# Linear attention with decay, then an MLP: group 0 scaled from SBUF, group 3 turned by TensorE, four output buffers, a new written order

## The chip, the cores and the metric

The kernel runs on one core of one Trainium2 chip. The metric is the device time of one execution in microseconds (us). A core has TensorE (PE, the matrix engine; its weight loads are shown as PEld), VectorE (DVE), ScalarE (ACT), GpSimd (POOL), SyncE (SP, which here only issues DMAs) and DMA engines that all queues share. The engines run at the same time; each executes its own list of instructions in order and waits only where data or a buffer isn't ready.

## The reference

`r`, `k`, `v` have the shape (4 sequences, 8 heads, 768 steps, 48); `w` and `u` have one value for each head and channel.

```
for t in range(S):
    cur     = outer(u * k[t], v[t])
    y[t]    = r[t] @ (state + cur)
    state   = w * state + outer(k[t], v[t])
x = y as (3072 tokens, 384)
h = x @ w_in                       # 384 -> 2048
g = h if h >= 1, 0 if h <= -1, else (h+1)^2/4
out = g @ w_out                    # 2048 -> 384
```

## The kernel before

**Tiling.** The 768 steps are cut into 6 chunks of 128 (`C`). The 4 sequences are taken two at a time (`UNITS = 2`). So there are 12 groups, `g = 2*chunk + pair`, and 24 units, `n = 2*g + j`; a unit is 128 tokens of one sequence with all 8 heads. Group 3 is the "fourth group": chunk 1, second pair of sequences.

**Attention of one group.** The recurrence over steps becomes matrix products inside a chunk. Loads of R, K and V (`LR`, `LK`, `LV`, issued by SP, line 252). R and K are scaled with powers of `w` that depend on the step (`Rs`, `Ks`, tables `Wup` and `Wdn`, line 271) and turned, so that channels lie on the partitions: either by TensorE (`TR`, `TK`, `T`, line 319) followed by a copy out of PSUM (`cR`, `cK`, `c`, line 111), or by a transposing DMA on SP's queue (`RT`, `KT`, line 307). `A` (line 359) are the products of turned K and turned R, `AT` the same under the triangular mask (DVE). `Y` (lines 421 and 427) adds `AT` times V and turned R times the state. The term with `u` goes by the diagonal: `KU = K*u`, `RKU = R*KU`, `us` sums it per head, `B` multiplies it with V (cast to bf16 by `V` on ACT), and `y`/`yg` adds it to `Y`. `Sp` (line 394) is the new part of the state, `Tm`/`Tmg` and `decayg` update the state, `sbf`/`sbfg` cast it to bf16.

**MLP of one group.** y is turned (`X` on TensorE with the copy `xc`, or `xcg` by a transposing DMA). `m g.q` (line 464) is a quarter of the first product (12 matmuls), `r`, `s`, `g` are the activation (mostly ACT, ACT, DVE), `M g.jq` (line 499) a quarter of the second product for one unit (4 matmuls). `og` copies the result out of PSUM into a buffer `o`, `stg` stores it. `WI` and `WO` load the weights, cast to bf16 on the way, from POOL's queue.

**The start.** `ln`, `bw`, `WupS`, `WdnS` build the two tables in SBUF from `w`, and `Wup`, `Wdn` build the same in PSUM for group 0, so that group 0 can be scaled early. `bu`, `uS` spread `u`.

**The order** is written out by hand in `ORDER`: the program is emitted word by word, and each engine gets its instructions in that order. A word is the step, the group or unit, a letter for the engine after `=` (V is DVE, A is ACT, G is POOL), and after `/` the PSUM buffers: banks `b0` to `b3` for the first two groups' small tiles, pairs `p0`, `p1` from the beginning, and pairs `p2`, `p3` that take the place of the four banks later. Zn stands for n matmuls of zeros into a buffer that nobody reads.

**Buffers** are counted in `SLOTS`. The one that counts here is `"o": 2`: an `og` has to wait until the store of the `og` two before it has landed.

```
def do_Rs(e, b, g, j=None):
    t = flat(Wup) if g else tiles["up_t"]      # up_t: the table in PSUM
def do_og(e, b, g):
    copy(e, make("o", ("o", g), ...), tiles["op", g][:, :, :DO])
```

Of the kernel before, what the change touches and what calls it, by code (L numbers as in the profile page):

```python
# [21 lines left out]


ORDER = """
Zs/0 LK0.0 LR0.0 LK0.1 LR0.1 LR1.0 LR1.1 ln Z19 bw/2 WupS bu/1 Wdn/0 Ks0.1=V Wup/1 uS=A KU0.1=G Ks0.0=V Z5 TK0/3
Rs0.0=V TR0/1 cK0=V Rs0.1=V TK1/0 cK1=A RKU0.1=V LV0.0 LV0.1 KU0.0=V RKU0.0=G WdnS us0.1 cR0=A Z14 A0/23 us0.0 AT0.0
TR1/0 cR1=A Z4 A1/01 Rs1.1=V WI0 WI1 LK1.0 LK1.1 V0.0 wq/2 wE B0.0=G Rs1.0=G LV1.0 LV1.1 AT1.0 AT0.1 Z4 Y0/2 WI2 TR3/0
LK2.0 AT1.1 Ks1.0=G cR3=A Ks1.1=V Z6 TK3/1 cK3=V V0.1 B0.1=G LR2.0 LR2.1 V1.0 y0 TR2/3 cR2=V LK2.1 Z2 A3/01 AT3.0 X0/2
xc0=V KU1.1=G Y1/3 y1 KU1.0=G RKU1.0=G TK2/0 cK2=V Z2 X1/2 AT3.1 A2/30 AT2.1 wC=A Sp1/1 Tm1 xc1=A m0.0/0 r0.0=A s0.0=A
m0.1/1 r0.1=A LK3 us1.0 AT2.0 RKU1.1=G us1.1 Sp2/0 Tm2 LR3 Y2/0 V1.1 Sp3/1 s0.1=A B1.0=V Y3/3 y2 X2/2 xc2=A g0.0  # L30
m0.2/0 r0.2=A B1.1=G y3 X3/0 Sp0/2 g0.1 s0.2=A m0.3/1 r0.3=A s0.3=A Tm3 Tm0 xc3=V m1.2/3 m1.0/2 g0.2 WO0 WO1 Rs2=G
Ks2=G m1.1/0 r1.2=V g0.3 m1.3/1 KU2=G RKU2=G s1.2=A g1.2 LV2.0 LV2.1 LV3 M0.00/3 M0.10 M0.01 r1.0=A s1.0=A g1.0 r1.3=A
s1.3=A M0.11 g1.3 M1.00/2 sbf1=A sbf0=A M1.10 Rs3=G M0.12 M0.13 T4/1 r1.1=A s1.1=A M0.02 M0.03 Ks3=V KT3 KU3=G c4=A
T5/1 c5=A g1.1 us2 V2 B2=G A4/0 AT4 M1.11 RT3 LR4 LK4 A5/1 AT5 og0=A LR5 M1.12 M1.13 Y4/0 Y5 yg2 sbf2=A V3 RKU3=G
M1.01 AA3/13 AT6 X4/0 xc4=A M1.02 X5/0 xc5=A M1.03 og1=A LK5 AT7 Y6/1 m2.0/0 sbf3=A us3 Rs4=G RT4 Sp4/2 Sp5 Tmg2
r2.0=A s2.0=A B3=G Y7 yg3 xcg3 m2.1/3 r2.1=A m2.3/2 LV4 m2.2/1 Ks4=G KT4 g2.0 M2.00/0 M2.10 s2.1=A g2.1 M2.01 M2.11
LV6 r2.2=V m3.1/3 stg0 KU4=G RKU4=G LK6 LR6 r2.3=A s2.3=A s2.2=A decayg2=G g2.3 r3.1 m3.0/2 g2.2 M2.02 M2.03 Sp6/1 Sp7
us4 s3.1=A KU5=G M2.12 Ks5=G r3.0 g3.1 M2.13 s3.0=A KT5 Tmg3 og2=A Rs5=G m3.2/3 g3.0 LV5 V4 AA4/01 AT8 sbfg2=A
decayg3=G m3.3/2 RT5 AT9 B4=G M3.00/0 stg1 r3.2 s3.2=A M3.01 Y8/1 Y9 RKU5=G r3.3 g3.2 yg4 xcg4 s3.3=A V6 M3.10 M3.02
g3.3 KU6=G V5 sbfg3=A M3.11 LK10 stg2 us5 M3.12 M3.03 LR7 AA5/21 AT10 M3.13 Rs6=G og3=A m4.0/3 AT11 B5=G r4.0 LK7  # L40
m4.1/2 s4.0=A Y10/0 Y11 m4.2/1 r4.1 s4.1=A yg5 Ks6=G xcg5 RKU6=G m4.3/0 g4.0 RT6 M4.00/3 M4.10 r4.2 s4.2=A g4.1 Rs7=G
M4.11 Sp8/2 Sp9 KT6 M4.01 g4.2 LV7 LR8 M4.02 m5.1/1 LR9 r4.3 Tmg4 s4.3=A g4.3 decayg4=G us6 B6=G r5.1 KU7=G AA6/02
AT12 M4.03 LK8 sbfg4=A AT13 M4.12 M4.13 m5.0/0 s5.1=A RT7 g5.1 Ks7=G og4=A Y12/2 Y13 m5.2/1 r5.0 s5.0=A m5.3/3 yg6
xcg6 g5.0 RKU7=G Sp10/2 Sp11 r5.2 s5.2=A M5.00/0 M5.10 Ks8=G KT7 Tmg5 M5.11 LK9 decayg5=G g5.2 M5.01 M5.02 us7 m6.1/2
r5.3 s5.3=A g5.3 stg3 V7 LR11 B7=G r6.1 AA7/13 AT14 M5.12 KU8=G KT8 sbfg5=A s6.1=A M5.13 AT15 Rs8=G M5.03 og5=A m6.0/1
g6.1 LV8 r6.0 KU9=G RT8 s6.0=A Rs9=G Y14/3 Y15 Sp12/0 yg7 m6.2/2 m6.3/3 Sp13 xcg7 r6.2 stg4 g6.0 M6.00/1 s6.2=A Tmg6
decayg6=G r6.3 RT9 g6.2 M6.10 RKU8=G LR10 M6.11 Ks9=G M6.01 s6.3=A g6.3 stg5 M6.12 m7.1/0 AA8/32 M6.02 V8 r7.1 AT17
s7.1=A M6.13 KT9 M6.03 AT16 m7.0/2 sbfg6=A Sp14/3 Sp15 LV10 KU10=G us8 B8=G og6=A stg6 g7.1 r7.0 m7.2/1 s7.0=A Tmg7
LV9 Rs11=G g7.0 Y16/0 Y17 decayg7=G m7.3/3 yg8 r7.2 s7.2=A M7.00/2 xcg8 M7.10 Ks10=G r7.3 g7.2 s7.3=A g7.3 M7.11 M7.01
M7.02 V10 AA9/01 AT18 RT11 RKU9=G V9 M7.12 AT19 KT10 sbfg7=A M7.13 RKU10=G LK11 m8.0/3 Rs10=G M7.03 us9 r8.0 us10  # L50
og7=V s8.0=A g8.0 B9=G m8.1/1 r8.1 Y18/0 Y19 RT10 B10=G s8.1=A yg9 m8.2/2 r8.2 KU11=G xcg9 m8.3/3 s8.2=A g8.1 M8.00/0
LV11 M8.10 r8.3 M8.01 Sp16/1 g8.2 Sp17 Tmg8 M8.11 M8.12 stg7 m9.0/2 s8.3=A decayg8=G g8.3 AA10/31 AT21 M8.13 r9.0
M8.02 AT20 s9.0=A M8.03 m9.1/1 V11 sbfg8=A Y20/3 Y21 g9.0 Ks11=G og8=A yg10 xcg10 m9.2/0 r9.1 KT11 s9.1=A M9.00/3 r9.2
s9.2=A g9.1 m9.3/2 RKU11=G stg8 g9.2 M9.10 M9.11 r9.3 Sp18/1 Sp19 Tmg9 s9.3=A M9.01 M9.02 g9.3 decayg9=G us11 m10.0/0
r10.0 B11=G AA11/12 M9.12 M9.13 AT23 s10.0=A M9.03 sbfg9=A AT22 og9=V m10.1/2 stg9 Y22/1 Y23 g10.0 m10.2/3 r10.1
M10.00/0 s10.1=A r10.2 yg11 xcg11 g10.1 M10.10 m10.3/1 s10.2=A g10.2 r10.3 s10.3=A M10.01 M10.11 m11.1/2 M10.12 M10.02
g10.3 r11.1 m11.0/3 s11.1=A g11.1 M10.13 m11.2/1 r11.0 m11.3/2 s11.0=A r11.2 s11.2=A g11.0 M10.03 M11.10/3 og10=V
M11.11 r11.3 stg10 g11.2 M11.00/0 M11.01 M11.02 s11.3=A g11.3 M11.12 M11.13 M11.03 o11.1=A st11.1 o11.0=A st11.0
"""
# [14 lines left out]
def kernel(  # L74
# [193 lines left out]
    def product(e, out, a, b, g, j):  # L268
        j0, j1 = by_unit(g, j)
        part = lambda x: x.rearrange("p (b h) d -> p b h d", b=UNITS)[:, j0:j1]  # L270
        engines[e].tensor_mul(part(out)[:, :, :, :D], part(a), rep(b, j1 - j0) if len(b.shape) == 3 and b.shape[1] == H else part(b))  # L271
# [295 lines left out]
```

## Time and profile before

| | |
|---|---|
| three runs | 178.55 us median (178.06 to 178.93) |
| profiled execution | 177.88 us, of which the span from first to last instruction is 176.1 us |
| TensorE | 163.8 us busy (93%), 1638 matmuls, 1638 weight loads |
| DVE | 131.0 us busy (74%), 149 instructions |
| ACT | 129.3 us busy (73%), 150 instructions |
| POOL | 114.9 us busy (65%), 83 instructions |
| first product | 576 matmuls, 68.8 us; second product: 384 matmuls, 68.5 us |
| mean granted TensorE clock | 0.990 of full speed |

Busy time is the union of the spans of an engine's instructions. A matmul's span holds its way through the array, so spans overlap and the mean of one is more than what a matmul adds to a dense stream; what a stream takes is read from start to start. "Idle before, releaser" in a row says how long an engine stood before an instruction and what ended that.

### The profile page before, as it was taken

Reading aid. Unit: us, or ns where it says so; the run is one execution under the profiler, and the core shown is the slowest. Engines: PE = TensorE matmul, PEld = TensorE weight load, DVE = VectorE, ACT = ScalarE, POOL = GpSimd, SP = SyncE. Lnnn points to the kernel's source line nnn. Section 1 sums busy time; section 2 is a strip of 40 time slices with the busy share of each in tenths; the row PEclk is TensorE's granted clock in tenths of the full one; section 3 lists DMA queues with packets and bytes.
Section 4 is the critical chain, followed back from the end, with each engine's and each line's share of the span. In section 5 each row is a group of like instructions: output and inputs, shape, how many; then the busy total and the mean of one; then the engine's idle time right before and its main releaser. Section 6 shows DMA issues by size and latency. Waiting matters only on the chain.

```text
span 176.1 us, 3979 instructions
## 1 busy us (share of the span) xinstructions
PE 163.8 (93%) x1638; PEld 129.0 (73%) x1638; DVE 131.0 (74%) x149; ACT 129.3 (73%) x150; POOL 114.9 (65%) x83
## 2 busy tenths in 40 slices
...
GB/s 113 196 183 189 202 184 190 207 204 195 160 187 161 177 262 153 240 266 163 174 204 168 179 254 176 217 263 231 183 111 178 45 48 149 4 134 2 2 90 92
DMA packets 105703, 28.78 MB, mean 163 GB/s; under 512 B 100946, under 2 KB 104788, under 8 KB 105684
## 3 DMA queue, kind: packets, MB, share of 16 engines
...
q8 instruction: 13, 0.21, 0.6%
...
q10 hardware_dynamic: 4, 0.00, 0.0%
HBM read 20.45 MB, written 4.72 MB: 143 GB/s over the span
## 4 chain that ended last, share of the span: by engine, by line
PE 51%; DMA 20%; SPq 15%; ACT 4%; DVE 4%; issue 2%; POOL 1%; ACTq 0%; POOLq 0%
PE hp L464 25%; PE op L499 20%; SPq L252 14%; DMA Ri<-in_r_dram 8%; DMA out_dram<-o 8%; DMA RT<-Rs 2%; DVE g L487 2%; DMA xT<-y 2%; PE A L359 2%; ACT pt L475 2%; PE Y L427 2%; PE Y L421 1%; ACT sq L484 1%; PE Sp L394 1%; POOL Rs L271 1%
## 5 line engine op out<-in xcount | busy, mean ns | idle before, releaser
L487 DVE SCALAR_TENSOR_TENSOR g<-sq,hp 128x1024 bf16<-128x1024 bf16 x48 | 58.4, 1218 | 17.1 <-ACT sq L484 16.8
L464 PE MATMUL hp<-xT,w_in 128*128 128x256 bf16 x576 | 68.8, 273 | 1.0 <-DMA xT<-y 0.8
L499 PE MATMUL op<-w_out,g 128*128 128x384 bf16 x384 | 68.5, 326 | 0.2 <-DVE g L487 0.2
L464 PEld LDWEIGHTS <-w_in 128*128 128x128 bf16 x576 | 61.9, 114 | 4.5 <-DMA xT<-y 1.4
L475 ACT ACTIVATE pt<-hp 128x1024 f32<-128x1024 f32 x46 | 46.9, 1019 | 19.1 <-PE hp L464 19.1
L499 PEld LDWEIGHTS <-g 128*128 128x128 bf16 x384 | 35.9, 98 | 22.4 <-DVE g L487 1.2
L484 ACT ACTIVATE sq<-pt 128x1024 bf16<-128x1024 f32 x46 | 48.7, 1058 | 1.4
L368 DVE TENSOR_TENSOR AT<-A,umask 128x1024 bf16<-128x1024 f32 x20 | 23.6, 1220 | 8.2 <-PE A L359 8.0
L271 POOL TENSOR_TENSOR Rs<-Ri,Wup 128x768 bf16<-128x768 f32 (+1 forms) x11 | 19.4, 1760 | 9.7 <-DMA Ri<-in_r_dram 9.7
L271 POOL TENSOR_TENSOR KU<-Ki,u_sb 128x768 f32<-128x768 f32 (+1 forms) x13 | 21.2, 1635 | 4.7 <-ACT u_sb L111 4.7
L271 POOL TENSOR_TENSOR RKU<-Ri,KU 128x768 f32<-128x768 f32 (+1 forms) x13 | 21.2, 1638 | 1.9 <-DVE KU L271 1.7
L405 POOL TENSOR_TENSOR state<-Tm,wCm 128x768 f32<-128x768 f32 x8 | 14.6, 1831 | 11.7 <-DVE Tm L402 11.7
L302 POOL TENSOR_TENSOR V<-Vb,diag 128x768 f32<-128x768 bf16 (+1 forms) x13 | 17.2, 1330 | 5.6 <-ACT Vb L111 4.5
L271 POOL TENSOR_TENSOR Ks<-Ki,Wdn 128x768 bf16<-128x768 f32 (+1 forms) x10 | 17.9, 1786 | 2.2 <-DMA Ki<-in_k_dram 2.1
L439 DVE TENSOR_TENSOR y<-Y,V 128x768 bf16<-128x768 f32 x10 | 9.6, 956 | 5.7 <-POOL RKU L271 2.4
L293 DVE TENSOR_REDUCE diag<-RKU 128x16 f32<-128x768 f32 (+1 forms) x14 | 11.6, 831 | 0.6 <-POOL RKU L271 0.6
L111 ACT COPY o<-op 128x768 f32<-128x768 f32 (+1 forms) x10 | 7.4, 737 | 6.3 <-PE op L499 3.3
L111 ACT CAST Vb<-Vi 128x768 bf16<-128x768 f32 (+1 forms) x14 | 10.2, 736 | 1.5 <-DMA Vi<-in_v_dram 1.5
L427 PE MATMUL Y<-Vb,AT 128*128 128x48 bf16 x192 | 10.5, 185 | 0.6 <-DVE state L398 0.6
L427 PEld LDWEIGHTS <-AT 128*128 128x128 bf16 x192 | 9.3, 97 | 1.4 <-issue 0.8
L402 DVE TENSOR_TENSOR Tm<-Sp,state 128x768 f32<-128x768 f32 x8 | 7.6, 955 | 1.5 <-PE Sp L394 1.4
L111 ACT CAST state_bf<-state 128x768 bf16<-128x768 f32 (+1 forms) x12 | 8.5, 720 | 0.0
...
## 6 DMA issues: line engine op xcount, KB each, us to landing
...
w_out<-in_moe_w_out_dram POOLq DMA_DIRECT2D x2, 768.0 KB, 10.2
Ki<-in_k_dram SPq DMA_DIRECT2D x6, 192.0 KB, 4.7
Ri<-in_r_dram SPq DMA_DIRECT2D x6, 192.0 KB, 4.3
Vi<-in_v_dram SPq DMA_DIRECT2D x6, 192.0 KB, 4.6
```

The costliest lines, as they stand in the source:

```text
L111: nc.scalar.copy(out, in_) if e == "A" else engines[e].tensor_copy(out, in_)
L252: nc.sync.dma_start(out=t[:, j0 * H : j1 * H, :], in_=source(x, g, j0, j1))
L271: engines[e].tensor_mul(part(out)[:, :, :, :D], part(a), rep(b, j1 - j0) if len(b.shape) == 3 and b.shape[1] == H else part(b))
L302: engines[e].tensor_mul(t[:, hs, :], tiles["V", g][:, hs, :], tiles["diag", g][:, hs].unsqueeze(2).to_broadcast([P, n, D]))
L368: nc.vector.tensor_mul(t.rearrange("p i n t -> p (i n) t"), tiles["A", n].rearrange("p i (n t) -> p (i n) t", t=P), umask.unsqueeze(1).to_ ...
L405: engines[e].tensor_mul(states[g % BP], tiles["Tm", g], flat(wCm).unsqueeze(1).to_broadcast([P, UNITS, DM]))
L427: nc.tensor.matmul(Y[:, h * D : (h + 1) * D], AT[:, i, p, :], V[:, j * H + h, :], start=(c == 0), stop=True, skip_group_check=True,)
L464: nc.tensor.matmul(hp[:, f, :], w_in_sb[wi][:, i, wo * FG * P + f : (wo + 1) * FG * P : FG], tiles["xT", g][:, :, i, :], start=(i == 0), s ...
L475: nc.scalar.activation(t, tiles["hp", g, q], AF.Relu, bias=0.5, scale=0.5)
L484: nc.scalar.activation(t, p, AF.Square)
L487: nc.vector.scalar_tensor_tensor(out=make("g", ("g", g, q), [P, FG, TOK], BF16), in0=tiles["sq", g, q], scalar=1.0, in1=tiles["hp", g, q], ...
L499: nc.tensor.matmul(tiles[key][:, k, :DO], tiles["g", g, q][:, f, j * P : (j + 1) * P], w_out_sb[wi][:, wo, f * DO : (f + 1) * DO], start=( ...
```

## The change

- Group 0's `Rs` reads the table `Wup` in SBUF, since the word `Wup/1`, which made the copy of it in PSUM, is gone. `Ks` of group 0 still reads its table in PSUM.
- Group 3 (units 6 and 7) is turned by TensorE: `T6`, `T7`, copied by `c6`, `c7` on ACT. The two transposing DMAs `RT3` and `KT3` are gone.
- `"o"` has 4 buffers, not 2.
- The whole order is new. Idle matmuls: 67 (19, 4, 9, 7, 2, 7, 8, 3, 8), which were 56 (19, 5, 14, 4, 4, 6, 2, 2). Some steps have another engine: `RKU0.0`, `KU0.1`, `B0.0`, `Rs1.0`, `KU1.0`, `RKU2`, `KU3`, `cR3`, `xc2`, `xc4`, `xc5`, `og3`, `og6`, `r1.1` and `r2.3` are now on DVE; `RKU0.1`, `Ks1.1`, `B1.0` on POOL; `cK2`, `xc0`, `r2.2`, `og7` on ACT.

```
-Zs/0 LK0.0 LR0.0 LK0.1 LR0.1 LR1.0 LR1.1 ln Z19 bw/2 WupS bu/1 Wdn/0 Ks0.1=V Wup/1 uS=A KU0.1=G Ks0.0=V Z5 TK0/3
-Rs0.0=V TR0/1 cK0=V Rs0.1=V TK1/0 cK1=A RKU0.1=V LV0.0 LV0.1 KU0.0=V RKU0.0=G WdnS us0.1 cR0=A Z14 A0/23 us0.0 AT0.0
-TR1/0 cR1=A Z4 A1/01 Rs1.1=V WI0 WI1 LK1.0 LK1.1 V0.0 wq/2 wE B0.0=G Rs1.0=G LV1.0 LV1.1 AT1.0 AT0.1 Z4 Y0/2 WI2 TR3/0
 ...
+Zs/1 LV0.0 LR0.0 LR0.1 ln LK0.0 Z19 bw/3 bu/0 WupS LK0.1 V0.0 Rs0.0=V LV0.1 Rs0.1=V LR1.0 WdnS Wdn/2 Z4 TR1/1 uS=A
+TR0/3 cR0=A cR1=A KU0.0=V Ks0.0=V RKU0.0=V KU0.1=V Z9 TK0/1 cK0=V LV1.0 RKU0.1=G WI0 Ks0.1=V us0.0 B0.0=V LK1.0 Z7
+TK1/1 cK1=A LK1.1 A0/32 LR1.1 WI1 AT0.1 Z2 A1/10 LV1.1 LK2.0 wq/2 Rs1.0=V AT1.1 V0.1 V1.0 wE Ks1.1=G AT0.0 us0.1 Z7
+Y0/0 wC=A B0.1=G AT1.0 Z8 Y1/2 TK3/3 TR2/1 y0 LR2.0 y1 X0/0 Ks1.0=G LK2.1 xc0=A cR2=V WI2 Z3 X1/1 xc1=A KU1.0=V Sp1/2
+Rs1.1=V Z8 TR3/0 Tm1 TK2/1 cK2=A cK3=V m0.0/0 cR3=V RKU1.0=G KU1.1=G A2/20 Sp2/1 r0.0=A m0.1/1 RKU1.1=G AT2.0 s0.0=A
+Tm2 us1.1 AT2.1 g0.0 r0.1=A Y2/2 A3/31 us1.0 V1.1 s0.1=A Sp3/0 AT3.1 Sp0/1 AT3.0 B1.0=G y2 Y3/3 LR2.1 g0.1 WO0 m0.3/0
+LR3 B1.1=G y3 LK3 WO1 X2/2 xc2=V Ks2=G KU2=G r0.3=A X3/3 Tm0 m0.2/1 xc3=V s0.3=A r0.2=A Tm3 m1.1/2 g0.3 s0.2=A m1.2/3
+r1.1=V g0.2 m1.0/0 s1.1=A m1.3/1 g1.1 r1.0=A LV2.0 s1.0=A sbf2=A M0.00/2 r1.2=V g1.0 M0.10 M0.11 s1.2=A M0.01 r1.3=A
+Rs2=G T4/0 c4=A M0.12 M0.13 sbf0=A g1.2 RKU2=V LV2.1 M0.02 A4/3 us2 M0.03 s1.3=A Rs3=G og0=A sbf1=A M1.00/0 M1.01
+M1.10 T5/2 g1.3 Ks3=V LV3 LK4 c5=A M1.11 KU3=V AT4 LR5 M1.12 RKU3=G A5/1 M1.13 V2 AT5 LR4 T7/2 T6/3 sbf3=A Y4/1 Y5
+B2=G us3 c7=A M1.02 M1.03 yg2 KU4=G c6=A LV4 X4/2 Sp4/1 X5/3 og1=A xc4=V Sp5 A6/2 xc5=V LK5 V3 A7/0 m2.0/3 AT6 B3=G
+AT7 m2.1/2 r2.0=A Ks4=G Tmg2 Y6/0 Y7 s2.0=A yg3 RKU4=G m2.2/1 g2.0 r2.1=A xcg3 s2.1=A g2.1 m2.3/0 r2.2=A Rs4=G M2.00/3
+KU5=G M2.10 KT4 s2.2=A LK7 M2.11 V4 m3.1/2 r2.3=V RT4 g2.2 s2.3=A g2.3 r3.1 decayg2=G M2.01 m3.0/1 LV6 stg0 s3.1=A us4
+M2.12 Rs5=G g3.1 r3.0 LK6 Sp6/0 Sp7 M2.02 M2.03 Ks5=G s3.0=A M2.13 sbfg2=A Tmg3 AA4/20 g3.0 V6 KT5 AT8 RKU5=G m3.2/1
+og2=A RT5 AT9 Y8/2 r3.2 m3.3/3 us5 LV5 Y9 s3.2=A B4=G decayg3=G M3.00/0 r3.3 s3.3=A yg4 M3.01 g3.2 xcg4 M3.10 M3.11
 ...
+s10.1=A og9=V xcg11 m10.3/3 r10.2 g10.1 stg9 s10.2=A r10.3 g10.2 s10.3=A M10.00/0 M10.10 M10.11 M10.01 m11.1/1 g10.3
+m11.0/2 r11.1 M10.02 r11.0 m11.2/3 s11.1=A M10.12 s11.0=A g11.1 M10.13 M10.03 r11.2 g11.0 s11.2=A og10=V m11.3/1
+M11.10/2 stg10 g11.2 M11.11 r11.3 M11.00/0 M11.01 s11.3=A M11.12 g11.3 M11.02 M11.03 M11.13 o11.0=A st11.0 o11.1=A
+st11.1

-SLOTS = {... "xT": 3, "pt": 3, "sq": 3, "g": 13, "o": 2}
+SLOTS = {... "xT": 3, "pt": 3, "sq": 3, "g": 13, "o": 4}

 def do_Rs(e, b, g, j=None):
-        t = flat(Wup) if g else tiles["up_t"]
+        t = tiles["up_t"] if g == 0 and "up_t" in tiles else flat(Wup)
 def do_Ks(e, b, g, j=None):
-        t = flat(Wdn) if g else tiles["dn_t"]
+        t = tiles["dn_t"] if g == 0 and "dn_t" in tiles else flat(Wdn)
```

In the order before, the corresponding stretch of groups 2 to 4 reads, cut to what the prediction speaks of:

```
... Rs3=G M0.12 M0.13 T4/1 r1.1=A s1.1=A M0.02 M0.03 Ks3=V KT3 KU3=G c4=A
T5/1 c5=A g1.1 us2 V2 B2=G A4/0 AT4 M1.11 RT3 LR4 LK4 A5/1 AT5 og0=A LR5 ... Y4/0 Y5 yg2 sbf2=A V3 RKU3=G
M1.01 AA3/13 AT6 X4/0 ... LK5 AT7 Y6/1 m2.0/0 ... RT4 ... xcg3 ... LV4 ... KT4
LV6 ... stg0 ... LK6 LR6 ... og2=A ... KT5 ... Rs5=G m3.2/3 g3.0 LV5 V4 AA4/01 ... RT5
...
M11.11 r11.3 stg10 g11.2 M11.00/0 M11.01 M11.02 s11.3=A g11.3 M11.12 M11.13 M11.03 o11.1=A st11.1 o11.0=A st11.0
```

More of the change, by code (lines that the diff above doesn't have):

```diff
@@ L24 @@
 ORDER = """
-Zs/0 LK0.0 LR0.0 LK0.1 LR0.1 LR1.0 LR1.1 ln Z19 bw/2 WupS bu/1 Wdn/0 Ks0.1=V Wup/1 uS=A KU0.1=G Ks0.0=V Z5 TK0/3
-Rs0.0=V TR0/1 cK0=V Rs0.1=V TK1/0 cK1=A RKU0.1=V LV0.0 LV0.1 KU0.0=V RKU0.0=G WdnS us0.1 cR0=A Z14 A0/23 us0.0 AT0.0
-TR1/0 cR1=A Z4 A1/01 Rs1.1=V WI0 WI1 LK1.0 LK1.1 V0.0 wq/2 wE B0.0=G Rs1.0=G LV1.0 LV1.1 AT1.0 AT0.1 Z4 Y0/2 WI2 TR3/0
-LK2.0 AT1.1 Ks1.0=G cR3=A Ks1.1=V Z6 TK3/1 cK3=V V0.1 B0.1=G LR2.0 LR2.1 V1.0 y0 TR2/3 cR2=V LK2.1 Z2 A3/01 AT3.0 X0/2
-xc0=V KU1.1=G Y1/3 y1 KU1.0=G RKU1.0=G TK2/0 cK2=V Z2 X1/2 AT3.1 A2/30 AT2.1 wC=A Sp1/1 Tm1 xc1=A m0.0/0 r0.0=A s0.0=A
@@ L30 @@
[L30 to L58, printed above, removed]
+Zs/1 LV0.0 LR0.0 LR0.1 ln LK0.0 Z19 bw/3 bu/0 WupS LK0.1 V0.0 Rs0.0=V LV0.1 Rs0.1=V LR1.0 WdnS Wdn/2 Z4 TR1/1 uS=A
```

18 lines of the change are left out of this document (17 added, 1 removed).

## The prediction

> **What bounds the kernel now.** I read the page's shares first, then busy time by stretches, then TensorE's waits, then the timeline round each wait. The stretches:
>
> ```profile
> PE 163.8 (93%) x1638; PEld 129.0 (73%) x1638; DVE 131.0 (74%) x149; ACT 129.3 (73%) x150; POOL 114.9 (65%) x83
> ...
> 8.40:19.90 11.50, 9.64 (x121) 7.81 (x120) 10.16 (x20) 5.20 (x12) 10.03 (x11) 0.85 1.28 189
> 19.90:30.00 10.10, 8.26 (x97) 7.89 (x95) 8.53 (x15) 7.43 (x9) 6.27 (x7) 1.00 1.05 189
> 30.00:50.00 20.00, 19.15 (x196) 13.54 (x195) 15.35 (x15) 15.15 (x20) 12.05 (x8) 1.00 1.23 192
> 50.00:82.00 32.00, 30.26 (x316) 24.87 (x314) 23.71 (x23) 25.66 (x29) 29.26 (x18) 1.00 1.23 207
> 82.00:167.20 85.20, 84.42 (x852) 67.40 (x851) 65.98 (x62) 69.09 (x73) 54.73 (x32) 1.00 0.72 143
> ```
>
> The first row gives busy time and share of the whole span. The columns of the others are length, then busy time of PE, PEld, DVE, ACT and POOL, PE's granted clock, the DMA share and GB/s. From 82 us on TensorE stands for 0.78 us in 85.2: there the kernel is bound by its matmuls, whose number stays. An order can win only what TensorE loses before: 1.84 us in 19.9 to 30, 0.85 in 30 to 50, 1.74 in 50 to 82; further the time until the first product starts at 19.9 us, and the tail behind the last matmul. In 8.4 to 19.9 the fullest engine is DVE (10.16 of 11.5 us), so the start is set by DVE's list. TensorE's waits, two answers (19.9 to 82 us, then 82 to the end):
>
> ```profile
> PE A L359 <- DMA RT<-Rs: 1.5, 2, 0.8
> PE Sp L394 <- ACT Vb L111: 1.0, 1, 1.0
> PE A L359 <- ACT o L111: 0.8, 1, 0.8
> PE Y L427 <- DVE state L398: 0.6, 1, 0.6
> ...
> PE hp L464 <- DMA xT<-y: 0.6, 1, 0.6
> ```
>
> **The change part by part.** The profiled execution took 177.88 us, 1.78 more than its span of 176.1, and 0.67 less than the runs' median of 178.55. I sum against the execution and take the difference to the median.
>
> *Start: Rs of group 0, loads, idle matmuls, engines.* The rows:
>
> ```profile
> 6.48 0.50 ACT L111 COPY u_sb<-up 128x384 f32<-128x384 f32 x1
> ...
> 8.20 0.54 DVE L271 TENSOR_TENSOR Rs<-Ri,up_t 128x384 bf16<-128x384 f32 x1
> 8.65 0.55 DVE L271 TENSOR_TENSOR RKU<-Ri,KU 128x384 f32<-128x384 f32 x1
> ...
> 11.85 0.55 DVE L271 TENSOR_TENSOR Rs<-Ri,Wup 128x384 bf16<-128x384 f32 x1
> ...
> 12.31 1.88 DVE L373 TENSOR_TENSOR AT<-A,umask 128x512 bf16<-128x512 f32 x3
> ...
> 14.11 1.40 DVE L271 TENSOR_TENSOR Ks<-Ki,Wdn 128x384 bf16<-128x384 f32 x1
> 14.14 0.80 POOL L243 DMA_DIRECT2D w_in<-in_moe_w_in_dram  x1
> ...
> 14.97 1.39 POOL L271 TENSOR_TENSOR Ks<-Ki,Wdn 128x384 bf16<-128x384 f32 x1
> ...
> 19.90 2.78 PE L464 MATMUL hp<-xT,w_in 128*128 128x256 bf16 x24
> ...
> 24.49 1.21 DVE L487 SCALAR_TENSOR_TENSOR g<-sq,hp 128x1024 bf16<-128x1024 bf16 x1
> ...
> 25.75 1.47 PE L464 MATMUL hp<-xT,w_in 128*128 128x256 bf16 x12 [0.16 <-DVE g L487]
> ...
> 34.34 5.46 PE L499 MATMUL op<-w_out,g 128*128 128x384 bf16 x32
> ```
>
> Rs from SBUF costs 0.55 us as against 0.54 from PSUM: nothing. `uS` has one ACT instruction more ahead of it (`V0.0`, `WdnS`, `Wdn` for `Wdn`, `Wup`), so at about 0.5 us each it ends near 7.5 instead of 6.98, and `KU0.0` on DVE starts near 7.6. K0.0 moves from the first to the fourth place of SP's queue and K0.1 from the third to the fifth; by the landings of these places
>
> ```profile
> Ri<-in_r_dram SPq DMA_DIRECT2D x1, 192.0 KB, 4.2
> ...
> Ri<-in_r_dram SPq DMA_DIRECT2D x1, 192.0 KB, 4.4
> ```
>
> (us from issue, at 2.71 and 3.54) they land at 6.9 and 7.9: in time for 7.6 and for `KU0.1` near 9.0. From 7.6 DVE has no idle place in the new list. The SBUF instructions start 0.45 to 0.5 us apart (8.20, 8.65), `AT` 0.63 (1.88 / 3), copies about 0.4. Fourteen items to `y0` (`KU0.0`, `Ks0.0`, `RKU0.0`, `KU0.1`, `cK0`, `Ks0.1`, `us0.0`, `B0.0`, `AT0.1`, `Rs1.0`, `AT1.1`, `AT0.0`, `us0.1`, `AT1.0`): 10 x 0.45 to 0.5 + 4 x 0.63 = 7.0 to 7.5, `y0` at 14.6 to 15.1; then `y1`, `cR2`, `KU1.0`, `Rs1.1` until about 17.1, `TR3`, `TK2`, and m0.0 at about 17.6, 2.3 us earlier than 19.90. Most of that is lost again: ten items follow up to `AT3.0` (`Tm1`, two copies, `AT2.0`, `Tm2`, `us1.1`, `AT2.1`, `g0.0` of 1.21, `us1.0`, `AT3.1`), and A2 has to wait for m0.0, g0.0 for ACT; I get `AT3.0` done at 24.5, Y3, and m0.3 at 25.0, where m0.2 stood at 25.75. Then X3 waits for `y3`, m0.2 runs near 27.0, four m of 1.3 (two take 2.78 with the way through the array), and M0.00 comes at about 33.6 against 34.34. I take 0.7 us. Bounds: +2.3, if all of the early m0.0 stays; -0.9, if one DVE instruction is stretched as `Ks1.1` was (1.40 where 0.55 is usual, 0.85 more) and one POOL instruction delays what DVE waits for.
>
> The eleven more idle matmuls lie in TensorE's waits for DVE and cost nothing there; with cover gone they cost 11 x 0.1. The w_in parts: the third is moved behind `B0.1` and `Ks1.0` on POOL, from 14.14 to about 16.2.
>
> *T6, T7 for RT3, KT3.* The rows:
>
> ```profile
> 39.63 0.39 PE L319 MATMUL T<-ident,Rs 128*128 128x128 bf16 x4
> 39.85 0.39 PE L319 MATMUL T<-ident,Ks 128*128 128x128 bf16 x4
> ...
> 40.28 1.01 ACT L111 COPY TT<-T 128x1024 bf16<-128x1024 bf16 x1 [0.59 <-PE T L319]
> ...
> 47.09 0.62 PE L359 MATMUL A<-RT,KT 48*128 48x128 bf16 x16 [0.80 <-DMA RT<-Rs]
> ```
>
> Four transposes take 0.22 us (39.63 to 39.85), so sixteen add 0.9 us of matmuls; the wait of 0.80 us for RT3 goes. Net 0.1 us lost. Bounds: 0.9 lost if the new place waits as long; 0.8 won if the transposes fill a wait. `c6`, `c7` are two of 1.01 us on ACT, which has 4.85 us idle in 30 to 50; behind them on ACT stand `og1` and `V3`, and A7 (pair 0) waits for `og1`: with cover gone, up to 1.0. On SP two transposes go and LK4, LR5, LR4, LV4 move up. DVE takes `RKU2`, `KU3` from POOL; idle in 30 to 50: 4.65 us.
>
> *Four output buffers.* The rows:
>
> ```profile
> 57.30 2.51 SPq L307 DMA_TRANSPOSE KT<-Ks  x1
> ...
> 60.53 1.43 SPq L518 DMA_DIRECT2D out_dram<-o  x1
> ...
> 65.33 0.80 ACT L111 COPY o<-op 128x768 f32<-128x768 f32 x1 [1.37 <-DMA out_dram<-o]
> ...
> 66.18 0.62 PE L359 MATMUL A<-RT,KT 48*128 48x128 bf16 x16 [0.83 <-ACT o L111]
> ...
> 166.32 6.01 PE L499 MATMUL op<-w_out,g 128*128 128x384 bf16 x36
> ...
> 172.77 0.48 ACT L111 COPY o<-op 128x384 f32<-128x384 f32 x1 [0.57 <-DMA out_dram<-o]
> ```
>
> The first store was issued at 60.53, `og2` waited for it to land, and A of group 4 waited 0.83 us for `og2`, whose PSUM it takes. With four buffers `og2` waits for no store: 0.8 us. Next late there would be KT4, issued at 57.30 behind RT4 and eight us before A. Bounds 0 to 0.8. At the end `o11.0` no longer waits 0.57 us; the last matmuls end at 166.32 + 6.01 = 172.33, so the copy can start 0.4 us earlier.
>
> *SP's queue before A of group 5.* The rows:
>
> ```profile
> 67.86 1.54 SPq L252 DMA_DIRECT2D Vi<-in_v_dram  x1
> ...
> 69.51 2.28 SPq L307 DMA_TRANSPOSE RT<-Rs  x1
> ...
> 74.44 0.62 PE L359 MATMUL A<-RT,KT 48*128 48x128 bf16 x16 [0.69 <-DMA RT<-Rs]
> ```
>
> RT5 stood behind LV5 (1.54 us); in the new order LV5 comes after it, and A of group 5 stands later. 0.7 us, bounds 0 and 0.7; if `Rs5` on POOL is late, nothing, as POOL is the fullest engine but TensorE there (29.26 of 32).
>
> *From 82 us.* Other order, same work; DVE gets one `og` more. Zero. Bounds: 0.8 won (the idle time there), 1.7 lost (that of the stretch before it, the nearest).
>
> Sum: 0.7 - 0.1 + 0.8 + 0.7 + 0.4 = 2.5 us. 177.88 - 2.5 = 175.4 for the execution, 178.55 - 2.5 = **176.0** for the median.
>
> **The rivals.**
>
> *Given back (no change).* DVE's list, not m0.0, sets M0.00 and the 0.7 goes; A of group 4 or 5 waits for POOL's `Ks4`, `Rs4`, `Rs5` instead. For it: POOL's 29.26 of 32 us, and that `Ks3` on DVE waits for K3, which now lands behind R3:
>
> ```profile
> 40.12 1.82 POOL L271 TENSOR_TENSOR Rs<-Ri,Wup 128x768 bf16<-128x768 f32 x1 [5.62 <-DMA Ri<-in_r_dram]
> ```
>
> R3 had this last place and landed at 40.1; K3 there would hold `Ks3`, `KU3`, `AT4`, `AT5` on DVE. Against: `Ks3` is due only near 40 in my walk, and POOL loses `RKU2` and `KU3`. Left are the tail's 0.4 and perhaps half of 0.8, less 0.1: 177.8.
>
> *DVE and POOL hold each other up (slower).* At 14.11 a DVE product with both operands in SBUF took 1.40 us beside POOL, and POOL's own 1.39. The change puts `KU1.0` beside `Ks1.0`, `Rs1.1` beside `RKU1.0`, `RKU2` beside `Rs3`, all such pairs. Price: 0.85 for each of the first two, and up to a whole POOL instruction, 1.82, for the third: 3.5 us of DVE's list. If all of it is on the path, 2.5 won turns into 1.0 lost: 179.5. It decides once more than 2.5 of it is on the path. Against: POOL waits for `KU1.0` before `RKU1.0`, for R3 before `Rs3`, so the pairs need not meet, and DVE has slack after 30.
>
> The Trainium skill (page "SBUF — State Buffer", section "Who interferes with whom") says that a VectorE instruction with two SBUF inputs and a GpSimd instruction that reads SBUF exclude each other, the later one waiting for the earlier. The row at 14.11 fits it; by that rule each pair that meets costs in full, which is this rival.
>
> *Late w_in.* The third part, issued at 14.14, landed 10.4 us later, at 24.5:
>
> ```profile
> w_in<-in_moe_w_in_dram POOLq DMA_DIRECT2D x1, 768.0 KB, 10.4
> ```
>
> If its landing moves with its issue, m0.3 waits from 25.0 to 26.6: 1.6 of the 2.5 is gone, 177.6. Against: two parts stand ahead of it in the same queue, so it may land as before. I count it with "given back".
>
> **How the numbers follow.** Forecast (1.3 to 4.5 us won, 174.0 to 177.2): 0.63. Given back or late weights (177.2 to 178.8): 0.21. Slower by the DVE and POOL pairs: 0.16. The low end is 2.3 at the start, 0.8, 0.7, 0.4 and some of the steady 0.8, with 0.1 to 0.5 lost: 4.5. The high end, 178.8, leaves out most of the slower case. About 0.5% (0.9 us) is what a measurement of this kernel can tell from no change: faster than 177.65, the forecast and a part of the second, 0.67; within, 0.19; slower, 0.14.
>
> **What would show it.** The first product starts at 17 to 18.5 us and M0.00 before 34; no wait of A for a transposing DMA at 47; no `og` that waits for a store, neither at 65 nor at the end; A of group 4 near 64 without a wait. I am wrong if TensorE waits longer for DVE between m0.0 and M0.00 (`KU1.0`, `Rs1.1` longer than 0.55), if A of group 4 or 5 waits for POOL's products, or if TensorE's idle time after 82 us grows over 2.

## The result, and the profile after

The changed kernel takes 176.01 us (median of 4 runs, 175.91 to 176.28), the kernel before 178.49 (4 runs, 178.06 to 178.93): a ratio of 0.9864 [0.9836, 0.9891], 2.5 us faster. The forecast was 176.0. The profiled execution took 176.28 us, its span 174.5. Line numbers of the changed kernel are one higher than before. Runs that took over 1.5% longer than the fastest of their kernel are left out of all ratios, so where the runs of a kernel scatter, its ratio and the median of all its runs differ, and both are given there.

The page's shares:

```profile
PE 166.0 (95%) x1665; PEld 132.5 (76%) x1665; DVE 135.6 (78%) x157; ACT 128.8 (74%) x147; POOL 109.2 (63%) x79
```

TensorE does 27 more matmuls (16 transposes, 11 idle ones), is busy for 166.0 instead of 163.8 us, and stands for 8.5 us of the span instead of 12.3. So between these two executions the gain is idle time of TensorE, 3.8 us less, of which 2.2 go into a longer busy time; 1.6 us of span are left (the profiled execution before took 0.6 us less than the median of its runs, the changed one 0.3 more). Not all of the 2.2 is added work: in 8.4 to 19.9 us TensorE is busy 1.4 us longer than before, with 117 matmuls where 121 stood. Where the idle time went shows in the stretches of the prediction (length, then busy time of PE, PEld, DVE, ACT, POOL, granted clock, DMA share, GB/s):

```profile
8.40:19.90 11.50, 11.06 (x117) 9.74 (x115) 9.66 (x21) 3.90 (x11) 7.43 (x9) 1.00 1.30 201
19.90:30.00 10.10, 7.77 (x98) 6.65 (x96) 8.77 (x16) 6.59 (x8) 6.55 (x7) 1.00 1.13 199
30.00:50.00 20.00, 20.00 (x206) 15.02 (x206) 17.85 (x18) 16.11 (x21) 10.68 (x7) 1.00 1.13 193
50.00:82.00 32.00, 31.62 (x347) 26.31 (x343) 27.56 (x27) 26.04 (x29) 29.11 (x17) 1.00 0.94 167
82.00:165.50 83.50, 82.80 (x838) 66.59 (x836) 65.14 (x61) 68.44 (x72) 53.81 (x32) 1.00 0.74 152
```

In 30 to 82 us TensorE now stands for 0.38 us where it stood for 2.59. In 19.9 to 30 it stands for 2.33 us, more than before (1.84), and after 82 us for 0.70 (0.78). TensorE's waits, 19.9 to 82 us and then to the end (what for: us in total, times, longest):

```profile
PE Sp L395 <- DVE AT L374: 1.0, 1, 1.0
PE Y L428 <- DVE AT L374: 1.0, 2, 0.7
PE hp L465 <- DMA xT<-y: 0.4, 1, 0.4
...
PE A L360 <- DMA KT<-Ks: 0.7, 2, 0.4
```

A's waits for RT of groups 3 and 5 and for ACT's `og2` are gone. Left are, above all, waits for DVE's `AT` between the first products. The timeline at the places that the prediction named:

```profile
7.42 0.56 DVE L272 TENSOR_TENSOR KU<-Ki,u_sb 128x384 f32<-128x384 f32 x1 [0.71 <-ACT u_sb L112]
...
12.54 1.86 PE L233 MATMUL wp<-ones,lnw 1*128 1x1 f32 x8
...
14.33 0.93 PE L527 MATMUL z<-idle 128*128 128x128 bf16 x7
...
15.05 0.53 PE L428 MATMUL Y<-Vb,AT 128*128 128x48 bf16 x8
...
18.45 0.55 DVE L272 TENSOR_TENSOR Rs<-Ri,Wup 128x384 bf16<-128x384 f32 x1
...
18.62 1.24 POOL L272 TENSOR_TENSOR RKU<-Ri,KU 128x384 f32<-128x384 f32 x1 [1.35 <-DVE KU L272]
...
19.56 1.47 PE L465 MATMUL hp<-xT,w_in 128*128 128x256 bf16 x12
...
35.26 2.76 PE L500 MATMUL op<-w_out,g 128*128 128x384 bf16 x16
...
61.92 1.65 SPq L519 DMA_DIRECT2D out_dram<-o  x1
...
64.80 0.62 PE L360 MATMUL A<-RT,KT 48*128 48x128 bf16 x16
...
66.20 0.79 ACT L112 COPY o<-op 128x768 f32<-128x768 f32 x1
...
72.80 0.62 PE L360 MATMUL A<-RT,KT 48*128 48x128 bf16 x16
...
171.03 0.48 ACT L112 COPY o<-op 128x384 f32<-128x384 f32 x1 [0.17 <-PE op L500]
```

Here M0.00 comes at 35.26, later than before (34.34). From M0.00 to the end of the span the kernel before took 141.8 us, the changed one 139.2. So in this execution the whole gain lies behind the start, and the start lost 0.9. The two executions do not start alike, though; the last experiment compares like with like.

### The profile page after: what moved, and what is told of

Read it like the earlier page. It is cut to its first block, busy times and chain, and to the rows that moved or that the text cites. A ratio compares the mean times of both kernels' runs of the same rounds, so it can differ in the third digit from the quotient of the medians.

```text
span 174.5 us, 4024 instructions
## 1 busy us (share of the span) xinstructions
PE 166.0 (95%) x1665; PEld 132.5 (76%) x1665; DVE 135.6 (78%) x157; ACT 128.8 (74%) x147; POOL 109.2 (63%) x79
## 4 chain that ended last, share of the span: by engine, by line
PE 79%; DVE 6%; DMA 6%; POOL 5%; issue 1%; ACT 1%; SPq 1%; DVEq 0%
PE op L500 30%; PE hp L465 30%; PE A L360 4%; DMA KT<-Ks 3%; PE z L527 3%; DMA Ri<-in_r_dram 2%; PE Y L428 2%; DVE g L488 2%; PE Y L422 2%; PE Sp L395 2%; POOL state L406 1%; DVE AT L374 1%; PE TK L320 1%; POOL RKU L272 1%; PE wp L233 1%
## 5 line engine op out<-in xcount | busy, mean ns | idle before, releaser
L476 ACT ACTIVATE pt<-hp 128x1024 f32<-128x1024 f32 x45 | 45.9, 1021 | 18.0 <-PE hp L465 17.9
L485 ACT ACTIVATE sq<-pt 128x1024 bf16<-128x1024 f32 x45 | 47.5, 1058 | 1.3
L272 POOL TENSOR_TENSOR RKU<-Ri,KU 128x768 f32<-128x768 f32 (+1 forms) x12 | 19.7, 1640 | 17.1 <-DVE KU L272 16.8
L272 POOL TENSOR_TENSOR Ks<-Ki,Wdn 128x768 bf16<-128x768 f32 (+1 forms) x11 | 18.4, 1674 | 2.7 <-DMA Ki<-in_k_dram 1.4
L272 POOL TENSOR_TENSOR Rs<-Ri,Wup 128x768 bf16<-128x768 f32 x10 | 18.3, 1829 | 0.7 <-DMA Ri<-in_r_dram 0.7
L272 POOL TENSOR_TENSOR KU<-Ki,u_sb 128x768 f32<-128x768 f32 (+1 forms) x10 | 17.4, 1744 | 2.0 <-DMA Ki<-in_k_dram 2.0
L112 ACT COPY o<-op 128x768 f32<-128x768 f32 (+1 forms) x9 | 6.5, 726 | 5.3 <-PE op L500 5.3
L527 PE MATMUL z<-idle 128*128 128x128 bf16 x67 | 8.4, 300 | 1.2 <-DVE idle L134 1.2
```

The costliest lines, as they stand in the source:

```text
L112: nc.scalar.copy(out, in_) if e == "A" else engines[e].tensor_copy(out, in_)
L476: nc.scalar.activation(t, tiles["hp", g, q], AF.Relu, bias=0.5, scale=0.5)
L485: nc.scalar.activation(t, p, AF.Square)
L527: nc.tensor.matmul(tiles["z"][:, 0, :P], idle[:, :P], idle[:, :P], start=True, stop=True)
```

## The experiments

"Before" and "after" name the kernel whose order is edited. Theories: the prediction's division (start 0.7, buffers 1.2 with the tail, RT5 0.7, turning group 3 on TensorE -0.1) against one cause, namely that RT3 and KT3 held up SP's queue and so everything that SP issued behind them.

**Four buffers alone (before).**

```
-"g": 13, "o": 2}
+"g": 13, "o": 4}
```

> The order before, with four output buffers and nothing else. Theory (each wait removed is a gain of its own): og2 no longer waits 1.37 us for the first store, A of group 4 no longer 0.83 us for og2, the last copy no longer 0.57 us; 0.8 + 0.4 = 1.2 us, so 177.3. Rival (the gain is taken up by the next wait): A of group 5 waits for RT5, which lands near 74.4 us whatever TensorE does, so its wait grows from 0.69 to about 1.5 us and only the tail's 0.4 us is left: 178.1.

Measured: ratio 1.0031 [0.9994, 1.0067], no gain. The median of all twelve runs is 179.41, 0.85 us above before. In the timeline of that kernel (an execution of 179.0 us span, 1.4 us over the median) `og2` no longer waits for a store, but:

```profile
65.83 4.27 SPq L307 DMA_TRANSPOSE KT<-Ks  x1
...
70.83 2.37 SPq L307 DMA_TRANSPOSE RT<-Rs  x1
...
75.67 0.62 PE L359 MATMUL A<-RT,KT 48*128 48x128 bf16 x16 [2.25 <-DMA RT<-Rs]
```

The 0.83 us at A of group 4 is taken up nine us later by A of group 5, which now waits 2.25 us (0.69 before) for RT5, issued at 70.83 (69.51 before). SP's queue is next late, not ACT. The direction is the one that the rival expected; the size is not like for like, since this execution started 1.1 us later than the profiled one before (the first product at 21.04 instead of 19.90).

**The transposing DMAs back in the changed order (after).**

```
-T7/2 T6/3 ... c7=A ... c6=A ... A6/2 ... A7/0
+RT3 ... KT3 ... AA3/20
```

> The order after, with group 3 turned by two transposing DMAs again (sixteen transposes and two copies less, KT3 behind Ks3, RT3 behind it on SP's queue). Theory (the terms as predicted): 0.9 us of matmuls less, a wait of A of group 3 of about 0.8 us more: 176.1, within 0.4 of the changed kernel. Rival (SP's queue is what T6 and T7 relieve): the DMAs wait for Ks3, which ends at 43.0, and hold up four loads behind them; A of group 3 waits longer than 1.5 us and later groups too: 177 or more.

Measured: 181.24 us, ratio 1.013 [1.0071, 1.0188]: without T6 and T7 the new order is slower than the kernel before, as the rival had it. Its timeline and stretches of two us:

```profile
50.70 0.62 PE L360 MATMUL A<-RT,KT 48*128 48x128 bf16 x16 [2.09 <-DMA RT<-Rs]
51.25 4.48 PE L465 MATMUL hp<-xT,w_in 128*128 128x256 bf16 x24
```

```profile
51.00:53.00 2.00, 2.00 (x21) 1.47 (x16) 1.86 (x2) 0.00 (x0) 2.00 (x2) 0.61 1.16 218
53.00:55.00 2.00, 2.00 (x12) 1.45 (x10) 1.35 (x2) 1.05 (x2) 1.54 (x2) 0.53 1.38 201
```

A of group 3 waits 2.09 us for RT3, and then the granted clock is 0.61 and 0.53 for four us: 24 matmuls of the first product take 4.48 us where 2.81 is usual (at 50.44 in the changed kernel). The wait costs nearly twice its length.

**Idle matmuls ahead of Y0 and Y1 taken out (after).**

```
-us0.1 Z7 Y0/0 ... AT1.0 Z8 Y1/2
+us0.1 Y0/0 ... AT1.0 Y1/2
```

> The order after without the seven idle matmuls ahead of Y0 and the eight ahead of Y1. In the changed kernel matmuls took about twice the time of a full clock until 18.5 us, the seven ended at 15.26 and the eight at 16.43, and Y0 and Y1 stood behind them though their AT were done at 14.15 and 15.21. Theory (idle matmuls on the path): y1 comes 1.0 us earlier, m0.0 near 18.6, and the time is 175.2. Rival 1 (DVE's list sets M0.00): m0.0 earlier, M0.00 still near 35.2, 176.0. Rival 2 (they keep the clock up): TensorE stays at half speed beyond 18.5 us and the first products take 2.6 instead of 1.3 us: 177.

Measured: ratio 0.9926 [0.9873, 0.9979], which rests on five of twelve runs: two took 175.8 and 175.9 us, eight 177.7 to 179.9, and two (214.2 and 574.3) lie far outside. That is no gain: the kernel of the next experiment, on the same chip, has 0.9888. The profiled execution is the one of 214 us, whose granted clock falls to 0.75 from 18 us on. Up to there it starts as the first execution of the changed kernel does, and Y1 begins at 15.30 instead of 16.23:

```profile
15.30 0.50 PE L428 MATMUL Y<-Vb,AT 128*128 128x48 bf16 x8 [0.43 <-DVE AT L374]
```

So in that start the idle matmuls did hold up Y1, by 0.93 us. Why the whole does not get faster without them stays open.

**m0.3 ahead of Sp0 and Y3 (after).**

```
-Sp3/0 AT3.1 Sp0/1 ... g0.1 WO0 m0.3/0
+Sp3/0 m0.3/0 AT3.1 Sp0/1 ... g0.1 WO0
```

> The order after with m0.3 ahead of Sp0 and Y3 on TensorE. In the changed kernel TensorE waited 0.96 and 0.27 us for AT ahead of Sp0 and Y3, and m0.3 stood behind them until 26.66, though its PSUM was free at 24.73 and its weights landed at 25.0. Theory (the order of TensorE's list costs it there): m0.3 starts near 25.0, M0.00 about 1.2 us earlier, 174.8. Rival (DVE's list sets M0.00): X3 waits for y3 as before, longer by what was won; 176.0.

Measured: 176.25 us, ratio 0.9888 [0.9844, 0.9932], as the changed kernel on the other chips (0.9807 to 0.9864). Its timeline:

```profile
25.21 1.50 PE L465 MATMUL hp<-xT,w_in 128*128 128x256 bf16 x12 [1.41 <-DMA w_in<-in_moe_w_in_dram]
```

m0.3 put earlier waits 1.41 us for the third part of w_in, which lands at 25.2, and M0.00 comes at 34.56. So "late w_in" was near the path, but covered by the waits for `AT`.

**T6 and T7 alone (before), then with four buffers, then also with LV5 behind RT5.**

```
-KT3 ... RT3 ... Y4/0 Y5 yg2 ... AA3/13
+T7/3 T6/1 Y4/0 Y5 c7=A c6=A yg2 ... A6/1 A7/3
 second kernel: also "o": 4
 third kernel: also g3.0 LV5 ... RT5  ->  g3.0 ... RT5 LV5
```

> The order before with units 6 and 7 turned by TensorE and copied by ACT, RT3 and KT3 gone, nothing else. Theory 1 (only the wait of A of group 3 counts): 0.9 us of transposes for a wait of 0.80 us: 178.5. Theory 2 (SP's queue is relieved): later transposing DMAs come earlier too, A of group 5 no longer waits 0.69 us for RT5: 177.8.

> The order before with units 6 and 7 turned by TensorE and four output buffers. Theory 2: the buffers' 0.8 us at A of group 4 is no longer taken up by RT5, and the tail gives 0.4: 176.7. Rival (the wait for RT5 takes it up, as with the buffers alone): 177.8 to 178.3.

> As the one before, and LV5 moved behind RT5 on SP's queue: the three parts in the old order. Theory (these parts are the gain): no wait of A of groups 3, 4 and 5, 176.3, as the changed kernel. Rival (the new order itself is the gain, by an earlier start and DVE's and POOL's lists): 177.5 or more.

Measured, all on one chip: 0.9896 [0.9845, 0.9947], 0.9886 [0.9827, 0.9946] and 0.9892 [0.9852, 0.9933]. By the ratio T6 and T7 alone give 1.9 us (1.04% of 178.46; 0.9 to 2.8 by the interval). That ratio rests on four of six runs; the median of all six, 177.23, is 1.2 us below before. Both are more than theory 1 (none) and theory 2 (0.7) expected. Buffers and LV5 add nothing that can be measured, but the runs scatter (175.57 to 180.12 us with the buffers, median 178.09; 175.17 to 178.02 with LV5 too, median 176.73), so that 0.7 us more or less could hide in that, and the two expectations for the buffers are not told apart. In the timeline of the kernel before, SP's queue between group 3 and group 4 reads:

```profile
39.64 2.85 SPq L307 DMA_TRANSPOSE KT<-Ks  x1
42.59 1.25 SPq L307 DMA_TRANSPOSE RT<-Rs  x1
43.89 1.05 SPq L252 DMA_DIRECT2D Ri<-in_r_dram  x1
```

R4 can only be issued when KT3 and RT3 are out, 4.2 us after KT3's turn came. The timeline with T6 and T7 alone:

```profile
39.60 1.76 SPq L252 DMA_DIRECT2D Ri<-in_r_dram  x1
...
58.84 1.56 SPq L518 DMA_DIRECT2D out_dram<-o  x1
...
63.60 2.47 SPq L307 DMA_TRANSPOSE KT<-Ks  x1
...
64.50 0.80 ACT L111 COPY o<-op 128x768 f32<-128x768 f32 x1
...
65.71 0.62 PE L359 MATMUL A<-RT,KT 48*128 48x128 bf16 x16
...
66.80 4.19 SPq L307 DMA_TRANSPOSE RT<-Rs  x1
...
73.43 0.62 PE L359 MATMUL A<-RT,KT 48*128 48x128 bf16 x16 [0.37 <-DMA RT<-Rs]
```

R4 is issued at 39.60 instead of 43.89, the first store at 58.84 instead of 60.53, and `og2` waits for nothing, with two buffers; the turn of RT5 comes 2.7 us earlier (69.51 before), though it is out only 0.8 us earlier (70.99 and 71.79), and A of group 5 waits 0.37 instead of 0.69 us.

**T6 and T7 with RT3 and KT3 left in the queue, read by nobody (before).**

```
 ... KT3 ... RT3 ...
-Y4/0 Y5 yg2 ... AA3/13
+T7/3 T6/1 Y4/0 Y5 c7=A c6=A yg2 ... A6/1 A7/3
```

> The kernel before, with T6, T7, c6, c7 added as in the changed kernel, so that A of group 3 reads what TensorE turned; but RT3 and KT3 stay in SP's queue too, and nobody reads what they write. So the transposes are there without the relief of SP's queue. Theory (the gain of T6/T7 comes from SP's queue, which two transposing DMAs and their wait for Ks3 and Rs3 no longer hold up): RT4 and KT4 are issued near 51 and 57, the first store at 60.5, og2 waits for it, A of group 4 waits 0.8 us, A of group 5 0.7 us for RT5; the time is that of the kernel before within 0.7 us (177.8 to 179.0). Rival (the gain comes from A of group 3, which no longer waits for RT3): the time is as with T6/T7 alone, 176.6 to 177.3.

Measured: 177.80 us, before 178.87 on that chip, ratio 0.9963 [0.9931, 0.9995]: by the ratios the transposes without the relief of the queue gain about 0.7 us, a third of what T6 and T7 alone gained. The times don't settle it: the intervals overlap (0.9931 to 0.9947), and by the medians of all runs the two gain nearly the same (1.1 and 1.2 us). The timeline says more:

```profile
47.25 0.62 PE L359 MATMUL A<-TT 48*128 48x128 bf16 x16 [0.18 <-ACT TT L111]
...
60.20 1.27 SPq L518 DMA_DIRECT2D out_dram<-o  x1
...
64.86 0.81 ACT L111 COPY o<-op 128x768 f32<-128x768 f32 x1 [0.70 <-DMA out_dram<-o]
...
65.72 0.62 PE L359 MATMUL A<-RT,KT 48*128 48x128 bf16 x16 [0.16 <-ACT o L111]
...
69.34 2.85 SPq L307 DMA_TRANSPOSE RT<-Rs  x1
...
74.36 0.62 PE L359 MATMUL A<-RT,KT 48*128 48x128 bf16 x16 [1.07 <-DMA RT<-Rs]
```

A of group 3 no longer waits for RT3, but the store goes out at 60.20 and RT5 at 69.34 as in the kernel before, `og2` waits 0.70 us for the store (and A of group 4 then only 0.16 for `og2`, where 0.8 was expected), and A of group 5 1.07 us for RT5. The stretch from 50 to 82 us, first of this kernel, then of T6 and T7 alone (there without the other engines):

```profile
50.00:82.00 32.00, 30.14 (x318) 24.84 (x315) 23.54 (x23) 25.55 (x29) 28.61 (x17) 1.00 1.15 204
```

```profile
50.00:82.00 32.00, 31.15 (x333) 1.00 1.13 190
```

In 30 to 50 TensorE stands for 0.23 us in both (0.85 before), in 50 to 82 for 1.86 here and 0.85 with T6 and T7 alone (1.74 before). The executions of these three kernels start alike; from M0.00 to the end they take 141.8 us (before), 141.4 (here) and 140.7 (T6 and T7 alone). So in the traces both effects are there, the wait of A of group 3 and the queue, the queue being the larger (0.7 of 1.1 us); with one execution of each, the sizes are not settled.

**RT3 and KT3 on ACT's queue (before).**

```
-nc.sync.dma_start_transpose(out=t, ...)
+(nc.scalar if g == 3 else nc.sync).dma_start_transpose(out=t, ...)
```

> The kernel before with its two transposing DMAs of group 3 (RT3, KT3) issued from ACT's queue instead of SP's, at the same words of the order; no T6, T7. So SP's queue is relieved without any transposes on TensorE. Theory (SP's queue): LR4 is issued near 39.6 instead of 43.89, RT4 near 49, the first store before 59, og2 does not wait for it, A of group 5 waits under 0.4 us; most of the gain of T6/T7 alone comes back, 176.6 to 177.8, if the transposes on the other queue are not slower than RT3 was. Rival (the transposes on TensorE matter by themselves): A of group 3 still waits 0.8 us or more, and the time stays within 0.7 us of the kernel before.

Measured: 181.15 us, ratio 1.0106 [1.0049, 1.0163], slower. A miss for the time, and it separates little: beside the loads, which now went past them, RT3 landed only 7.5 us after its issue and KT3 6.3 (in the kernel before these take 4.8 in the median). The group of DMA issues, two waits and a stretch:

```profile
RT<-Rs ACTq DMA_TRANSPOSE x1, 7.5
```

```profile
42.45 0.38 PE L319 MATMUL T<-ident,Rs 128*128 128x128 bf16 x4 [1.93 <-ACT TT L111]
...
50.84 0.62 PE L359 MATMUL A<-RT,KT 48*128 48x128 bf16 x16 [3.48 <-DMA RT<-Rs]
```

```profile
53.00:55.00 2.00, 2.00 (x18) 1.27 (x17) 1.49 (x2) 1.08 (x2) 0.36 (x1) 0.50 1.43 193
```

A of group 3 waits 3.48 us and the clock falls to 0.50 behind it. Before that TensorE stood 1.93 us for the copy `c4`, which in ACT's list stands behind the issue of KT3 (40.04 to 41.34): issuing the DMAs from ACT held up ACT's own work. Further on, no A waits and `og2` doesn't either, though with everything some 4 us later this is weak evidence for the queue.

**Three loads moved in SP's queue (after), the attempt at a faster version.**

```
-LV5 Y9 ... LR6 ... LR10 ... LK8 ... KT6
+LV5 LR6 Y9 ... KT6 LR10 LK8
```

> The changed kernel with three loads moved in SP's queue: R6 ahead of the transposing DMA of y of group 4, R10 and K8 behind KT6. It tries for a version that is faster than both. In the changed kernel SP issues without a gap from 64 to 100 us, and TensorE waits 0.37 for xT at 74.5, 0.32 for KT at 86.6 and 0.38 for KT at 110.8. If SP's queue is what sets these waits, the first two go and RT6 is issued near 79 instead of 82.3: 0.3 to 0.7 us faster than the changed kernel. Rival (POOL, busy 29.1 of 32 us there, is next late, or the loads that are put back are): the same within 0.3 us.

Measured: 182.93 us, ratio 1.0169 [1.0098, 1.0239], 7 us slower than the changed kernel. Its timeline (an execution of 182.3 us span, 1.1 us over the median):

```profile
70.00 1.62 SPq L253 DMA_DIRECT2D Ri<-in_r_dram  x1
71.72 2.56 SPq L457 DMA_TRANSPOSE xT<-y  x1
...
76.59 2.72 PE L465 MATMUL hp<-xT,w_in 128*128 128x256 bf16 x12 [2.19 <-DMA xT<-y]
```

```profile
78.00:80.00 2.00, 2.00 (x11) 1.26 (x9) 0.00 (x0) 0.66 (x1) 1.86 (x2) 0.57 0.00 0
```

R6 ahead of xT delayed xT's issue by 1.45 us (70.27 in the changed kernel, where its wait was 0.37), TensorE waited 2.19, and then the clock was at 0.57 (12 matmuls in 2.72 us, usual 1.47). A second wait of this kind, 2.76 us, followed at 102.81. The theory that SP's queue sets these waits holds, the idea that room was left in it doesn't.

**The changed kernel again, on two other chips.**

> The changed kernel once more, as the measure for the others of this call: 0.986 of the kernel before. Its first product starts near 18.4 us where idle matmuls had the clock up by 11 us, and near 19.6 where they had not; M0.00 between 34.1 and 35.3.

> The changed kernel unaltered, for comparison on the same chip: ratio to the kernel before 0.986, and about 0.5 us faster than the kernel before with T6/T7 alone if the rest of the new order counts.

Measured: 0.9859 [0.9818, 0.9899] beside T6 and T7 alone at 0.9896, and 0.9807 [0.9751, 0.9862]. The rest of the new order is worth about 0.6 us by the first pair (176.13 against 176.73 for the old order with T6, T7, buffers and LV5), but the intervals overlap: not settled. Starts and spans of the profiled executions (us):

| kernel | `wq` matmuls | m0.0 | M0.00 | span | M0.00 to the end |
|---|---|---|---|---|---|
| before | 1.05 | 19.90 | 34.34 | 176.1 | 141.8 |
| before, T6 and T7, RT3 and KT3 left in | 1.05 | 19.93 | 34.32 | 175.7 | 141.4 |
| before, T6 and T7 alone | 1.10 | 20.02 | 34.41 | 175.1 | 140.7 |
| before, RT3 and KT3 on ACT's queue | 1.05 | 18.93 | 33.41 | 179.5 | 146.1 |
| before, four buffers | 1.86 | 21.04 | 35.73 | 179.0 | 143.3 |
| before, T6, T7 and four buffers | 1.86 | 21.26 | 36.68 | 176.7 | 140.0 |
| before, T6, T7, four buffers, LV5 | 1.86 | 21.14 | 36.03 | 176.2 | 140.2 |
| after, first | 1.86 | 19.56 | 35.26 | 174.5 | 139.2 |
| after, again | 1.05 | 18.29 | 33.99 | 174.4 | 140.4 |
| after, third | 1.15 | 18.46 | 34.16 | 173.1 | 138.9 |

The same kernel starts in more than one way, and so does the old order, which none of its edits changes ahead of M0.00. In the first execution of the changed kernel the eight matmuls of `wq` took 1.86 us (the row at 12.54 above), in its second 1.05, as in the kernel before:

```profile
12.19 1.05 PE L233 MATMUL wp<-ones,lnw 1*128 1x1 f32 x8 [0.18 <-DVE AT L374]
```

Like for like, the new order brings m0.0 forward by 1.4 to 1.7 us in either start, and M0.00 by 0.2 to 0.4 where `wq` took 1.05 to 1.15 us, by 0.5 to 1.4 where it took 1.86. One execution of the old order is left out of this: its M0.00 at 33.41 (RT3 and KT3 on ACT's queue) is earlier than any of the new order, so how an execution starts moves M0.00 by more than the new order does. Even so, in the changed kernel M0.00 1.27 us earlier ended at 174.4 as against 174.5: TensorE's idle time in 82 to 120 us, where POOL is busy for 33.7 of 38 us, was 1.24 us in that execution and 0.70 in the first. What the earlier start is worth at the end is not settled.

## Why the prediction was right or wrong, point by point

The total was right (2.5 won, 2.5 measured), the division was not, so part of the hit is luck.

*Start, 0.7.* DVE's list ran as walked until `AT1.0`: `KU0.0` at 7.42 (walked: 7.6), the last `AT` done at 15.2. The step that failed first is that the eleven more idle matmuls "lie in TensorE's waits for DVE and cost nothing there": in the profiled execution wq and Z7 took about twice their time in front of Y0, which began at 15.05 where `AT0.0` was done at 14.15, and m0.0 came at 19.56, not 17.6. Where wq took 1.05 us, Y0 began at 13.86 with `AT0.0` done at 13.80, and m0.0 came at 18.29. The prediction's own row for 8.4 to 19.9 us shows a granted clock of 0.85, and its sum has no term for it. Taking Z7 and Z8 out brought no faster kernel, though: behind m0.0 `AT3.0` and w_in (25.2) come next, as "most of that is lost again" had it, and m0.3 stood at 25.4 to 25.6 in the two faster starts (walked: 25.0). Measured 0.2 to 0.4 in one kind of start, 0.5 to 1.4 in the other.

*T6, T7, -0.1.* This was the mis-sized term: in the old order +1.9 by the ratio, 1.2 by the median of all runs, 1.1 from M0.00 to the end in the traces. In the new order without them the kernel loses 4 to 5 us (181.24 against 176.25 for the kernel with m0.3 moved, on the same chip). The prediction set 0.9 us of transposes against a wait of 0.80 and noted that "on SP two transposes go and LK4, LR5, LR4, LV4 move up", but gave that move no price. The two DMAs held SP's queue from 39.64 to 43.84 and the loads behind them with it.

*Four buffers, 0.8, and RT5, 0.7.* Over-sized: the buffers alone gained nothing (1.0031 [0.9994, 1.0067]), and beside T6 and T7 neither could be measured, though intervals of over 1 us leave room for part of it. The waits were read rightly, their causes one step too short. `og2` waited for a store that stood late in SP's queue, and RT5 came late in the same queue; with T6 and T7 alone the first wait is gone and the second down to 0.37, and while the queue stays as it was the buffers gain nothing. LV5 was not moved by itself. The question "next late there would be KT4" was asked of A of group 4 alone, not of A of group 5. *The tail, 0.4:* the last copy waits for no store; the last matmul ends at 170.99, 3.5 us before the end of the span, where 3.8 stood before: 0.3.

*From 82 us, 0.* Right in sum (0.70 against 0.78 us idle; between 82 and 120 us 0.54 to 1.24 in three executions of the changed kernel).

*Rivals.* "DVE and POOL hold each other up": `RKU1.0` on POOL took 1.24 us beside `Rs1.1` (about 1.00 alone), `Rs1.1` itself 0.55, so the later instruction waited 0.24 us, on POOL, where it cost nothing. The rule of the Trainium skill (page "SBUF — State Buffer", section "Who interferes with whom") agrees with that row; the pairs hardly met, as the "against" had it. The row at 14.11, from which the price of 0.85 came, is less plain than it was read: POOL's `Rs1.0` ended at 14.20, and from 14.14 to 14.94 POOL issued the third part of w_in, no product. In the trace with RT3 and KT3 on ACT's queue the same `Ks1.1`, begun at 14.20 beside the same issue, took 0.55, in three others of the old order 2.02. What stretched it stays open. "Late w_in": the third part, issued 2.34 us later, landed at 25.0 instead of 24.5, as two parts stand ahead of it. "Given back" did happen to the start, but not to the later waits.
